# Attention and two feed-forward layers on one core: scores and P times V in one run each on TensorE, another order of first loads, a larger gap between weight tiles

## The chip, the core and the metric

The kernel runs on one core of a Trainium2 chip. Five engines work on their own queues, in order: TensorE (PE in the profile, with its weight loads as PEld), VectorE (DVE), ScalarE (ACT), GpSimd (POOL) and SyncE (SP), which here only issues DMAs. Times are device microseconds (us) of one execution. A comparison is between medians of several executions.

## What is computed

Sliding-window attention with a few global keys, a gated layer (w_in, w_out) and a second gated layer (w_gate, w_val, w_out). Batch 2, 8 heads, 768 tokens of 64 numbers per head; 1536 tokens of 512 numbers go through the layers. The reference, cut:

```python
def _attn_ref(q, k, v, n_global, n_local):
    scores = scale * np.matmul(q, k.transpose(0, 1, 3, 2))
    is_global = pos[None, :] < int(n_global)              # 8
    is_local = (rel >= 0) & (rel < int(n_local))          # 96
    keep = is_global | is_local
    scores = np.where(keep, scores + bias, -1000000000.0) # bias: slope of the head times distance
    a = np.exp(scores - np.max(scores, axis=-1, keepdims=True))
    a = a / (np.sum(a, axis=-1, keepdims=True) + 1e-09)
    return np.matmul(a, v)

def _moe_ref(x, w_in, w_out):
    h = x @ w_in
    return (h * (1.0 / (1.0 + np.exp(-h)))) @ w_out       # w_in 512 x 2048

def _moe2_ref(x, w_gate, w_val, w_out):
    gate = 1.0 / (1.0 + np.exp(-(x @ w_gate)))            # 512 x 1536
    return (gate * (x @ w_val)) @ w_out
```

The inputs are 64-bit numbers in memory; the kernel takes them as pairs of words or as 32-bit copies.

## The kernel before

**Attention.** Queries are cut into 12 blocks of 128 tokens (gi), each with four pairs of heads (p); n = 4 gi + p counts the pairs, and a slot m is two pairs, n = 2m and 2m + 1. Keys of a block and of the one before are all that a block needs. For a pair, `emit_T` transposes keys and queries on TensorE (L339) and copies them into kT on VectorE or ScalarE (L350, L352), with the head's scale. `emit_QK` multiplies queries and keys (L376): each head of the pair has 64 rows, so one head works in the upper and one in the lower half of the array's rows, into two PSUM banks. `soft` adds the mask and takes the maximum on VectorE (L391), the exponential on ScalarE (L398), divides by the sum (L404, L405 on VectorE, L407 on GpSimd). `emit_PT` transposes the result (L424) and copies it (L428). `emit_PV` multiplies with v (L445): each head has 64 columns of output, so the two heads work in two halves of the array's columns. Once all four pairs of a block are done, `take` copies the block into x as a high and a low part (L462 on ScalarE, L463 on VectorE) and issues the next load of v.

**Layers.** Products use the full array in three passes of high and low parts (`mm3`, L493, and L668, L670 later). Weights come as 64-bit numbers, 512 KB a tile, in three stage buffers (L173); `split_w` turns a tile into a high and a low part: L153 on ScalarE, L154, L155 and L158 on VectorE, L166 on ScalarE, L167 on VectorE. L155, L158 and L167 read two SBUF tiles. Sixteen weight tiles fit in at first.

**Order.** The program first runs the loads and masks (`load_qk`, `load_n`, `make_n`, `make_mask0`, `make_mask1`), then `run_att` with the first six slots of attention and no products, then `window`, which deals products and attention into each other by the table PLAN, then `phase_rest` with products alone. After each piece `unit` advances a counter; `pump_w` writes a `split_w` when at least `wst["gap"]` units (5) have passed since the last. What stands in the program is not yet the order on the engines: a scheduler takes all of it, keeps what depends on what, and fills each engine's queue in the order in which it estimates the inputs and the engine to be free, earlier program text first. In the first products (`window`) 256 tokens are done at a time: the first half needs the copies of blocks 0 and 1, the second half those of blocks 2 and 3.

In a head's first unit, `head`, the P times V of the slot two earlier come first and then the scores. Before, they were free pieces for the scheduler. While TensorE has nothing, `warm_up` multiplies zeros (L883) in the first 20 units.

Of the kernel before, what the change touches and what calls it, by code (L numbers as in the profile page):

```python
# [31 lines left out]
def attn_moe_moe2_kernel(  # L32
# [15 lines left out]
    B, H, S, D = q.shape  # L48
# [34 lines left out]
    def run_due():  # L83
        while True:
            due = [d for d in deferred if d[0] <= clock[0]]
            if not due:
                return
            d = min(due, key=lambda e: (e[0], e[1]))
            deferred.remove(d)
            d[2]()  # L90
# [7 lines left out]
    def unit():  # L98
        clock[0] += 1
        pump_w()  # L100
        run_due()
# [34 lines left out]
    wst = {"dma": 0, "split": 0, "on": False, "last": -100, "gap": 5, "wait": 8}  # L136
# [44 lines left out]
    def pump_w():  # L181
        if not wst["on"]:
            return
        n = wst["split"]
        if n < wst["dma"] and clock[0] >= wtime[n] + wst["wait"] and clock[0] >= wst["last"] + wst["gap"]:
            split_w(n)
            wst["split"] = n + 1
            wst["last"] = clock[0]
        n = wst["dma"]
        if n < len(wsrc) and n - wst["split"] < 3 and slot_free(n):  # L190
            dma_w(n)
            wst["dma"] = n + 1
# [27 lines left out]
    def load_n():  # L220
        raw = ap1.tile([128, 2, 2], I32, name="nraw")
        nc.sync.dma_start(out=raw[:, 0, :], in_=n_global.bitcast(I32).partition_broadcast(128))
        nc.scalar.dma_start(out=raw[:, 1, :], in_=n_local.bitcast(I32).partition_broadcast(128))
        return raw
# [73 lines left out]
    qk_t = {}  # L298
    v_t = {}

    def load_qk(gi):
        if gi >= NBLK:
            return
        b, s0 = gi // BLK, gi % BLK * 128
        t = qk_p.tile([128, 2, H, D], F32, tag="qk", name="qk")
        for h0, h1 in ((0, 2), (2, H)) if gi == 0 else ((0, H),):
            if gi == 0 and h0 == 2:
                qk_t["n"] = load_n()
            for j, src in enumerate((k, q)):
                eng = nc.scalar if gi == 0 and j else nc.sync  # L310
                eng.dma_start(
                    out=t[:, j, h0:h1], in_=src[b, h0:h1, s0:s0 + 128, :].rearrange("h p d -> p h d")
                )
        qk_t[gi] = t
# [16 lines left out]
    def emit_T(n):  # L331
# [28 lines left out]
        if p == NP - 1:  # L360
            load_qk(gi + 2)

    def emit_QK(n):
        gi, p = divmod(n, NP)
        if gi >= NBLK:
            return
        s, i = gi % 2, gi % BLK
        kt = kT[p]
        u, m = n % 2, n // 2
        sp = [bk["SA"][m % len(bk["SA"])], bk["SB"][m % len(bk["SB"])]]  # L370
        w = 128 if i == 0 else 256
        sp = [x[:, u * 256:u * 256 + w] for x in sp]
        for e in range(2):
            r = slice(64 * e, 64 * e + 64)
            rhs = kt[r, s, :] if i == 0 else kt[r, 0:2, :].rearrange("p a b -> p (a b)")
            nc.tensor.matmul(sp[e], kt[r, 2, :], rhs, start=True, stop=True)  # L376
        return sp

    def soft(n, sp):
        if sp is None:  # L380
            return
        gi, p = divmod(n, NP)
        s, i = gi % 2, gi % BLK
        w = 128 if i == 0 else 256
        t = t_p.tile([128, 2, 256], F32, tag="t", name="t")
        t_t[n] = t
        c = 2.0 ** -(2 * p + 1)
        m0 = 0 if i == 0 else (128 if s == 0 else 256)
        ss = ssum[n % 4]
        for e in range(2):  # L390
            nc.vector.tensor_tensor_reduce(  # L391
                t[:, e, 0:w], sp[e], mask[e][:, m0:m0 + w], op0=ALU.add, op1=ALU.min,
                scale=-c, scalar=3.0e38, accum_out=nm_all[:, gi, 2 * p + e:2 * p + e + 1],
            )

        def exps():
            for e in range(2):
                nc.scalar.activation(  # L398
                    out=t[:, e, 0:w], in_=t[:, e, 0:w], func=AF.Exp, scale=-1.0,
                    bias=nm_all[:, gi, 2 * p + e:2 * p + e + 1], accum_out=ss[:, e:e + 1],  # L400
                )

        def norm():
            nc.vector.tensor_scalar(ss, ss, 1.0e-9, None, op0=ALU.add)  # L404
            nc.vector.reciprocal(ss, ss)  # L405
            for e in range(2):
                nc.gpsimd.tensor_scalar(  # L407
                    t[:, e, 0:w], t[:, e, 0:w], ss[:, e:e + 1], 1.0, op0=ALU.mult, op1=ALU.mult
                )

        defer(1 + n % 2, exps)
        defer(2 + n % 2, norm)

    def emit_PT(n):
        gi, p = divmod(n, NP)
        if n < 0 or gi >= NBLK:
            return
        i = gi % BLK
        nk = 1 if i == 0 else 2
        t = t_t.pop(n)  # L420
        ps = bk["PT"][n % len(bk["PT"])]
        for e in range(2):
            for c in range(nk):
                nc.tensor.transpose(  # L424
                    ps[:, (e * nk + c) * 128:(e * nk + c + 1) * 128], t[:, e, c * 128:(c + 1) * 128], ident
                )
        pt = pt_p.tile([128, 512], F32, tag="pt", name="pt")
        nc.scalar.activation(out=pt[:, 0:256 * nk], in_=ps[:, 0:256 * nk], func=AF.Copy)  # L428
        pt_t[n] = pt

    def emit_PV(n):
        gi, p = divmod(n, NP)
        if n < 0 or gi >= NBLK:
            return
        s, i = gi % 2, gi % BLK
        pt = pt_t.pop(n)
        ps = bk["PV"][gi % len(bk["PV"])]
        if i == 0:
            vs = [v_t[gi]]
        else:  # L440
            vs = [v_t[gi], v_t[gi - 1]] if s == 0 else [v_t[gi - 1], v_t[gi]]
        nk = len(vs)
        for c in range(nk):
            for e in range(2):
                nc.tensor.matmul(  # L445
                    ps[64 * e:64 * e + 64, p * 128:(p + 1) * 128],
                    vs[c][:, (2 * p + e) * D:(2 * p + e + 1) * D],
                    pt[:, (e * nk + c) * 128:(e * nk + c + 1) * 128],
                    start=(c == 0),
                    stop=(c == nk - 1),  # L450
                )

    def take(n):
        gi, p = divmod(n, NP)
        if n < 0 or gi >= NBLK or p < NP - 1:
            return
        i = gi % BLK
        ps = bk["PV"][gi % len(bk["PV"])]
        g, j = divmod(gi, BPG)
        xs = slice(j * 128, (j + 1) * 128)  # L460
        pv = ps.rearrange("p (a b) -> p a b", a=NP)
        nc.scalar.activation(out=X[g][:, 0, :, xs], in_=pv, func=AF.Copy)  # L462
        nc.vector.tensor_tensor(X[g][:, 1, :, xs], pv, X[g][:, 0, :, xs].bitcast(F32), ALU.subtract)  # L463
        if 0 < i < BLK - 1:
            nc.sync.dma_start(
                out=v_t[gi][0:N_GLOB, :].rearrange("p (h d) -> p h d", h=H),
                in_=v[gi // BLK, :, 0:N_GLOB, :].rearrange("h p d -> p h d"),
            )
        load_v(gi + 2)

    def att_units(m0, m1):
        def head(n):
            emit_PV(n - 4)
            emit_PV(n - 3)
            sp = [emit_QK(n), emit_QK(n + 1)]
            take(n - 3)
            soft(n, sp[0])
            soft(n + 1, sp[1])

        for m in range(m0, m1):  # L480
            n = 2 * m
            yield lambda n=n: head(n)
            yield lambda n=n: emit_PT(n - 2)
            yield lambda n=n: emit_T(n + 2)
            yield lambda n=n: emit_PT(n - 1)
            yield lambda n=n: emit_T(n + 3)
# [122 lines left out]

    def run_att(n0, n1):  # L610
        wst["on"] = True
        for j, u in enumerate(att_units(n0, n1)):
            u()
            if j < 20:
                warm_up(1)
            unit()

    def phase_rest(prev):
        tasks = [("A1", NG - 1, c) for c in halves1[0]]
# [261 lines left out]
    def warm_up(n):  # L881
        for _ in range(n):
            nc.tensor.matmul(bank[4][:, 256:512], warm[:, 0:128], warm, start=True, stop=True)  # L883

    with ExitStack():
# [16 lines left out]
                  H=[bank[5], bank[6]], Y=[bank[7]])  # L902
# [45 lines left out]
```

## Time and profile before

| | us |
|---|---|
| median of three runs | 702.73 (699.41 to 702.90) |
| the profiled execution, whole | 700.78 |
| its span, first to last instruction | 698.9 |
| TensorE busy in the span | 680.9 |
| VectorE busy | 376.3 |
| ScalarE busy | 278.1 |
| GpSimd busy | 90.7 |

The profile's chain of waits is followed back from the last instruction: 93% of the span in it is TensorE. The time before the first product (41 us) is where TensorE has holes; the attention's slots then run until about 210 us beside products, and the rest is products. TensorE's figure of busy time counts matmuls that overlap, so two rows that both read 0.70 us may stand 0.63 apart; the distance from a start to the next start is the better measure, and the chain of waits gives it.

### The profile page before, as it was taken

How to read it: one execution, taken by the hardware profiler on the slowest of the kernel's cores; microseconds unless marked ns; L12 is line 12 of the kernel's file. 1: busy time of each engine (PE TensorE's matmuls, PEld its weight loads, DVE VectorE, ACT ScalarE, POOL GpSimd, SP SyncE). 2: the span in 40 equal slices, each digit the busy share in tenths (PEclk: the TensorE clock that was granted, in tenths of full speed). 3: DMA queues.
4: the chain of work that ended last, by engine and by line, in shares of the span. 5: the costliest groups of instructions: out<-in, count | busy, mean ns of one | idle time of the engine just before them, and what ended most of it. 6: DMA issues, size and time to landing. Idle time of an engine off the chain costs nothing.

```text
span 698.9 us, 9170 instructions
## 1 busy us (share of the span) xinstructions
PE 680.9 (97%) x3393; PEld 532.4 (76%) x3393; DVE 376.3 (54%) x861; ACT 278.1 (40%) x594; POOL 90.7 (13%) x174
## 2 busy tenths in 40 slices
PE   6899999999999999999999999999999999999995
PEld 4467776667767888888888888888888888888884
DVE  4899975635459999752389941311684211312212
ACT  3788755655446565432266521111352111111110
POOL 4455553342320000000000000000000000000000
PEclk9999999999999999999999999999999999999998
DMA  8676543110002554500025420000140000100101
GB/s 198 150 202 172 151 131 74 44 36 17 16 2 93 165 166 126 173 1 0 1 88 153 151 90 1 1 0 1 60 151 0 1 1 0 61 0 1 61 0 65
DMA packets 65268, 49.03 MB, mean 70 GB/s; under 512 B 39616, under 2 KB 60096, under 8 KB 65216
## 3 DMA queue, kind: packets, MB, share of 16 engines
q1 hardware_dynamic: 64016, 48.11, 24.0%
q8 instruction: 28, 0.46, 0.3%
q10 hardware_dynamic: 1200, 0.26, 0.2%
q14 instruction: 24, 0.20, 0.1%
HBM read 45.22 MB, written 3.15 MB: 69 GB/s over the span
## 4 chain that ended last, share of the span: by engine, by line
PE 93%; DVE 2%; ACT 2%; DMA 1%; issue 1%; POOL 0%; ACTq 0%; DVEq 0%
PE bank L493 55%; PE bank L670 14%; PE bank L668 13%; PE bank L376 4%; PE bank L445 3%; PE bank L424 3%; PE bank L339 2%; DMA nraw<-in_n_local_dram 1%; ACT t L398 1%; DVE t L391 0%; DVE acc L689 0%; ACT pt L428 0%; PE bank L883 0%; POOL t L407 0%; ACT u L153 0%
## 5 line engine op out<-in xcount | busy, mean ns | idle before, releaser
L493 PE MATMUL bank<-x,w 128*128 128x512 f32 (+1 forms) x1488 | 356.3, 389 | 0.6 <-ACT w L166 0.6
L493 PEld LDWEIGHTS bank<-x,w 128*128 128x128 f32 x1488 | 272.9, 188 | 65.7 <-issue 3.5
L530 DVE TENSOR_TENSOR sg<-sg,bank 128x512 f32<-128x512 f32 x36 | 24.7, 687 | 167.5 <-PE bank L493 167.5
L670 PE MATMUL bank<-w,g 128*128 128x512 f32 x432 | 104.5, 390 | 0.0
L670 PEld LDWEIGHTS bank<-w,g 128*128 128x128 f32 x432 | 81.1, 188 | 17.8
L668 PE MATMUL bank<-g,w 128*128 128x512 f32 x384 | 92.9, 390 | 0.0
L668 PEld LDWEIGHTS bank<-g,w 128*128 128x128 f32 x384 | 72.1, 188 | 15.9
L527 ACT ACTIVATE sg<-bank 128x512 f32<-128x512 f32 x36 | 21.5, 597 | 120.0 <-PE bank L493 119.9
L531 ACT ACTIVATE g<-sg 128x512 fp32r<-128x512 f32 x36 | 22.8, 633 | 93.1 <-DVE sg L530 93.1
L407 POOL TENSOR_SCALAR t<-t,ssum 128x256 f32<-128x256 f32 (+1 forms) x96 | 53.3, 573 | 42.0 <-DVE ssum L404 18.0
L493 PE MATMUL bank<-g,w 128*128 128x512 f32 (+1 forms) x240 | 55.0, 363 | 0.3 <-DVE acc L579 0.2
L166 ACT ACTIVATE w<-u 128x512 fp32r<-128x512 f32 x68 | 42.4, 630 | 32.1 <-DVE u L158 14.8
L153 ACT ACTIVATE u<-stage 128x512 f32<-128x512 f32 x68 | 45.3, 674 | 23.8 <-DVE w L167 18.7
L167 DVE TENSOR_TENSOR w<-u,w 128x512 fp32r<-128x512 f32 x68 | 46.5, 689 | 12.0 <-ACT w L166 11.7
L398 ACT ACTIVATE t<-t,nm_all 128x256 f32<-128x256 f32 (+1 forms) x96 | 46.1, 484 | 9.2 <-DVE nm_all L391 9.1
L155 DVE SCALAR_TENSOR_TENSOR u<-stage,u 128x512 int32<-128x512 int32 x68 | 48.7, 723 | 0.6
L158 DVE SCALAR_TENSOR_TENSOR u<-stage,u 128x512 int32<-128x512 int32 x68 | 47.9, 708 | 0.3
L493 PEld LDWEIGHTS bank<-g,w 128*128 128x128 f32 x240 | 37.9, 189 | 9.5 <-DVE acc L579 1.5
L391 DVE CUSTOM_DVE_ANT_0 t<-bank,mask 128x256 f32<-128x256 f32 (+1 forms) x96 | 33.3, 395 | 11.7 <-PE bank L376 10.3
L376 PE MATMUL bank<-kt 64*128 64x256 f32 (+1 forms) x192 | 37.0, 431 | 1.2 <-DVE kt L350 0.8
L518 ACT ACTIVATE g<-sg 128x512 fp32r<-128x512 f32 x48 | 30.2, 630 | 17.8 <-DVE sg L517 10.7
L517 DVE SCALAR_TENSOR_TENSOR sg<-sg,bank 128x512 f32<-128x512 f32 x32 | 21.9, 683 | 26.9 <-ACT sg L516 26.7
(89 smaller groups left out, 490.4 us busy)
## 6 DMA issues: line engine op xcount, KB each, us to landing
stage<-in_moe_w_out_dram SPq DMA_DIRECT2D x28, 512.0 KB, 4.0
stage<-in_moe_w_in_dram SPq DMA_DIRECT2D x16, 512.0 KB, 3.8
stage<-in_moe_w_gate_dram SPq DMA_DIRECT2D x12, 512.0 KB, 3.5
stage<-in_moe_w_val_dram SPq DMA_DIRECT2D x12, 512.0 KB, 3.5
v<-in_v_dram SPq DMA_DIRECT2D x12, 256.0 KB, 3.4
out_dram<-acc SPq DMA_DIRECT2D x12, 256.0 KB, 2.0
qk<-in_k_dram SPq DMA_DIRECT2D x11, 256.0 KB, 4.6
qk<-in_q_dram SPq DMA_DIRECT2D x11, 256.0 KB, 3.9
```

The lines of the kernel that those rows point to most:

```text
L153: nc.scalar.activation(out=st, in_=hw.bitcast(F32), func=AF.Copy, scale=2.0 ** -112)
L155: nc.vector.scalar_tensor_tensor(out=ui, in0=lw, scalar=29, in1=ui, op0=ALU.logical_shift_right, op1=ALU.bitwise_or)
L158: nc.vector.scalar_tensor_tensor(out=ui, in0=hw, scalar=-2 ** 31, in1=ui, op0=ALU.bitwise_and, op1=ALU.bitwise_or)
L166: nc.scalar.activation(out=w[:, 0, :], in_=st, func=AF.Copy)
L167: nc.vector.tensor_tensor(w[:, 1, :], st, w[:, 0, :].bitcast(F32), ALU.subtract)
L376: nc.tensor.matmul(sp[e], kt[r, 2, :], rhs, start=True, stop=True)
L391: nc.vector.tensor_tensor_reduce(t[:, e, 0:w], sp[e], mask[e][:, m0:m0 + w], op0=ALU.add, op1=ALU.min, scale=-c, scalar=3.0e38, accum_out= ...
L398: nc.scalar.activation(out=t[:, e, 0:w], in_=t[:, e, 0:w], func=AF.Exp, scale=-1.0, bias=nm_all[:, gi, 2 * p + e:2 * p + e + 1], accum_out ...
L407: nc.gpsimd.tensor_scalar(t[:, e, 0:w], t[:, e, 0:w], ss[:, e:e + 1], 1.0, op0=ALU.mult, op1=ALU.mult)
L493: nc.tensor.matmul(ps, wl[(slice(None), a) + wsl], xl[(slice(None), b) + xsl], start=(first and j == 0), stop=(last and j == len(order) - 1),)
L668: nc.tensor.matmul(yb[d], w[:, a, sl], gt[:, b, :], start=st, stop=en)
L670: nc.tensor.matmul(yb[d], gt[:, a, sl], w[:, b, :], start=st, stop=en)
```

## The change

Three edits. In `load_qk` the two word counts (n_global, n_local) are issued ahead of the first block's keys and queries, and these come in three pieces of heads (0 and 1, 2 and 3, 4 to 7) instead of two. In `head` the scores of both pairs and the P times V of two earlier pairs stand in a section in which the order on TensorE is the order of the text: scores of n + 1, scores of n, P times V of n - 3, P times V of n - 4. In `run_att` the gap between weight tiles is 9 units instead of 5.

```diff
--- before.py
+++ after.py
@@ load_qk
-        for h0, h1 in ((0, 2), (2, H)) if gi == 0 else ((0, H),):
-            if gi == 0 and h0 == 2:
-                qk_t["n"] = load_n()
+        if gi == 0:
+            qk_t["n"] = load_n()
+        for h0, h1 in ((0, 2), (2, 4), (4, H)) if gi == 0 else ((0, H),):
             for j, src in enumerate((k, q)):
                 eng = nc.scalar if gi == 0 and j else nc.sync
@@ att_units
         def head(n):
-            emit_PV(n - 4)
-            emit_PV(n - 3)
-            sp = [emit_QK(n), emit_QK(n + 1)]
+            with tc.manual_schedule(engines={mybir.EngineType.PE}):
+                sp = [emit_QK(n + 1), emit_QK(n)][::-1]
+                emit_PV(n - 3)
+                emit_PV(n - 4)
             take(n - 3)
@@ run_att
         wst["on"] = True
+        gap, wst["gap"] = wst["gap"], 9
         for j, u in enumerate(att_units(n0, n1)):
             u()
             if j < 20:
                 warm_up(1)
             unit()
+        wst["gap"] = gap
```

Three places in the queues show what moves. A row is a line of the program, the operation, output and inputs, and how many follow one another. kt_126 to kt_129 are the transposed keys and queries of head pairs 0 to 3; bank_76 and bank_77 take the scores of the two heads of a pair, bank_79 P times V; bank_78 and bank_80 the two kinds of transposes; x_87 is x for the first 512 tokens, w_93 to w_108 are the sixteen weight tiles, in the order of memory and not of use.

TensorE's queue in the first products, before:

```order
L424 MATMUL bank_78<-ident,t 128x128 x4
L445 MATMUL bank_79<-pt,v 64x128 x4
L493 MATMUL bank_82<-x_87,w_97 128x256 x7
L339 MATMUL bank_80<-ident,qk 128x128 x2
L376 MATMUL bank_76<-kt_126 128x256
L493 MATMUL bank_82<-x_87,w_97 128x256 x3
L493 MATMUL bank_82<-x_87,w_98 128x256 x8
L376 MATMUL bank_77<-kt_126 128x256
L493 MATMUL bank_82<-x_87,w_98 128x256 x4
L445 MATMUL bank_79<-pt,v 64x128 x4
L424 MATMUL bank_78<-ident,t 128x128 x4
```

The same stretch of TensorE's queue after:

```order
L494 MATMUL bank_82<-x_87,w_97 128x256 x9
L376 MATMUL bank_76<-kt_127 128x256
L376 MATMUL bank_77<-kt_127 128x256
L376 MATMUL bank_76<-kt_126 128x256
L376 MATMUL bank_77<-kt_126 128x256
L445 MATMUL bank_79<-pt,v 64x128 x8
L424 MATMUL bank_78<-ident,t 128x128 x4
L339 MATMUL bank_80<-ident,qk 128x128 x2
```

The scores of two pairs and the P times V of two pairs, each split up by products before, stand in one piece (x8 here is sixteen records of the profile, since each of these products makes two).

VectorE's queue around the copy of the first attention block into x (L463), before:

```order
L391 ISA t,nm_all<-bank_77,mask_125 128x256
L391 ISA nm_all 128x1
L167 TENSOR_TENSOR w_93<-u,w_93 128x512
L391 ISA t,nm_all<-bank_77,mask_125 128x256
L391 ISA nm_all 128x1
L350 TENSOR_SCALAR kt_129<-bank_80 128x256
L463 TENSOR_TENSOR x_87<-bank_79,x_87 128x4x128
```

And after:

```order
L154 TENSOR_SCALAR u<-u 128x512
L391 ISA t,nm_all<-bank_82,mask_125 128x256
L391 ISA nm_all 128x1
L391 ISA t,nm_all<-bank_82,mask_125 128x256
L391 ISA nm_all 128x1
L167 TENSOR_TENSOR w_97<-u,w_97 128x512
L155 SCALAR_TENSOR_TENSOR u<-stage,u 128x512
L463 TENSOR_TENSOR x_87<-bank_79,x_87 128x4x128
```

Before, the first weight tile (w_93) is finished just ahead of this copy; after, the fifth (w_97) is.

TensorE's queue up to the first product on tokens 256 to 511 (the last row but one before, the last row after), before:

```order
L376 MATMUL bank_77<-kt_129 128x256
L339 MATMUL bank_80<-ident,qk 128x128 x2
L445 MATMUL bank_79<-pt,v 64x128 x4
L424 MATMUL bank_78<-ident,t 128x128 x4
L493 MATMUL bank_83<-g,w_99 128x256 x3
L493 MATMUL bank_83<-g,w_100 128x256 x3
L493 MATMUL bank_83<-g,w_99 128x256 x3
L493 MATMUL bank_83<-g,w_100 128x256 x3
L339 MATMUL bank_80<-ident,qk 128x128 x2
L493 MATMUL bank_81<-x_87,w_93 128x256
L493 MATMUL bank_82<-x_87,w_97 128x256
```

And after:

```order
L376 MATMUL bank_77<-kt_128 128x256
L339 MATMUL bank_80<-ident,qk 128x128 x2
L445 MATMUL bank_79<-pt,v 64x128 x8
L424 MATMUL bank_78<-ident,t 128x128 x4
L339 MATMUL bank_80<-ident,qk 128x128 x2
L376 MATMUL bank_76<-kt_127 128x256
L376 MATMUL bank_77<-kt_127 128x256
L376 MATMUL bank_76<-kt_126 128x256
L376 MATMUL bank_77<-kt_126 128x256
L339 MATMUL bank_80<-ident,qk 128x128 x2
L494 MATMUL bank_81<-x_87,w_93 128x256
```

Before, twelve products of the half before stand between the block's last P times V and that product; after, those are done earlier, and a run of scores of the next slot stands there.

## Rows read from the trace of the kernel before

**Rows 1.** The page's first lines: span, busy time, share, instructions.

```profile
span 698.9 us, 9170 instructions
PE 680.9 (97%) x3393; PEld 532.4 (76%) x3393; DVE 376.3 (54%) x861; ACT 278.1 (40%) x594; POOL 90.7 (13%) x174
```

**Rows 2.** Busy time by windows: window, length, engines, TensorE clock, DMA share, GB/s.

```profile
20.00:30.00 10.00, 6.59 (x46) 3.71 (x46) 10.00 (x35) 7.72 (x24) 3.75 (x6) 0.97 0.63 161
...
42.00:60.00 18.00, 17.79 (x133) 13.65 (x133) 17.30 (x51) 14.95 (x40) 12.23 (x18) 1.00 0.65 184
60.00:80.00 20.00, 20.00 (x164) 15.44 (x163) 18.47 (x55) 15.18 (x39) 7.54 (x11) 1.00 0.56 154
...
100.00:120.00 20.00, 20.00 (x139) 14.44 (x138) 9.48 (x36) 9.82 (x29) 7.30 (x17) 1.00 0.36 85
```

**Rows 3.** Chain of waits, 42 to 71 us: start, length, engine, line, instructions.

```profile
43.92 1.02 PE bank L445 x16
...
48.08 0.63 PE bank L376 x4
...
50.51 0.59 PE bank L445 x8
...
52.35 0.63 PE bank L376 x2
...
66.55 0.37 PE bank L339 x2
...
68.09 1.44 PE bank L493 x12
69.53 0.22 PE bank L339 x2
69.75 0.23 PE bank L493 x2
```

**Rows 4.** VectorE's groups by line, 42 to 100 us: busy us, mean ns.

```profile
L155 DVE SCALAR_TENSOR_TENSOR u<-stage,u 128x512 int32<-128x512 int32 x12 | 10.7, 899 | 0.1
...
L158 DVE SCALAR_TENSOR_TENSOR u<-stage,u 128x512 int32<-128x512 int32 x12 | 9.9, 822 | 0.0
L167 DVE TENSOR_TENSOR w<-u,w 128x512 fp32r<-128x512 f32 x12 | 8.3, 690 | 0.0
```

**Rows 5.** The same view, 42 to 60 us.

```profile
L155 DVE SCALAR_TENSOR_TENSOR u<-stage,u 128x512 int32<-128x512 int32 x4 | 4.1, 1038 | 0.0
```

**Rows 6.** Timeline: start, length, engine, line, operation, output and input, idle before.

```profile
3.15 0.44 PEld L339 LDWEIGHTS bank<-ident,qk 128*128 128x128 f32 x2
...
10.65 0.28 DVE L391 CUSTOM_DVE_ANT_0 t<-bank,mask 128x128 f32<-128x128 f32 x1
...
18.16 0.49 DVE L154 TENSOR_SCALAR u<-u 128x512 int32<-128x512 int32 x1 [0.99 <-ACT u L153]
...
31.58 0.42 DVE L391 CUSTOM_DVE_ANT_0 t<-bank,mask 128x256 f32<-128x256 f32 x1 [1.53 <-PE bank L376]
...
38.04 0.75 DVE L154 TENSOR_SCALAR u<-u 128x512 int32<-128x512 int32 x2
...
39.65 0.67 DVE L155 SCALAR_TENSOR_TENSOR u<-stage,u 128x512 int32<-128x512 int32 x1
40.25 0.68 DVE L158 SCALAR_TENSOR_TENSOR u<-stage,u 128x512 int32<-128x512 int32 x1
...
57.12 1.28 POOL L520 TENSOR_TENSOR g<-sg,g 128x512 fp32r<-128x512 f32 x1
57.19 1.76 DVE L155 SCALAR_TENSOR_TENSOR u<-stage,u 128x512 int32<-128x512 int32 x1
...
69.69 0.68 DVE L463 TENSOR_TENSOR x<-bank,x 128x512 fp32r<-128x512 f32 x1
```

**Rows 7.** Chain of waits, first 12 us.

```profile
1.23 5.33 DMA nraw<-in_n_local_dram
...
6.66 0.18 DVE nf L229
```

## Prediction, before the changed kernel ran

> **What bounds the kernel now.** I read the page first, then the busy time by windows, then the chain of waits, then single rows of the timeline. The page has TensorE (PE) busy for 97% of the span [rows 1]; matmuls overlap in that figure, so the reader should look at what stands beside it. The windows [rows 2] show three stages. Early, TensorE has holes while VectorE is full (6.59 and 10.00 of 10 us from 20 to 30). From 42 us on TensorE is full (17.79 of 18, then 20.00 of 20), and up to 80 us VectorE nearly so (17.30 of 18, 18.47 of 20). After 100 us VectorE has half its time free (9.48 of 20) and TensorE alone is the bound. So time comes off in two ways: TensorE's queue needs less time for the same work, or the point from which it never waits again comes earlier. And early on a saving on TensorE can be eaten by VectorE, which has no room there.
>
> I cut the program at one point and call it S: the first product on tokens 256 to 511, which needs the fourth attention block (256 tokens are two blocks). In the chain it starts at 69.75 us [rows 3], as VectorE takes up that block's copy at 69.69 [rows 6]. Behind S I count TensorE work, ahead of S VectorE work.
>
> **Edit 1, the tied runs, behind S.** The scores use half of the array's rows, P times V half of its columns, and a change to or from the full array costs. In the chain [rows 3] eight P-times-V records take 0.59 us and sixteen in one run 1.02: the second eight cost 0.43, so entering and leaving costs 0.16 inside the run. The neighbours pay too: a pair of transposes takes 0.22 us, but 0.37 between two such runs, 0.15 more for one way out and one way in. A saved run of P times V is worth 0.16 + 0.15 = 0.31 us. A score pair takes 0.63 us; its two passes of 256 columns would stream in 0.43, by the rate of the second eight. So a saved run of scores is worth 0.20 + 0.15 = 0.35. A lone half of a pair (x2) also takes 0.63, as much as both halves (x4).
>
> In the order of TensorE's queue behind S there are 30 runs of scores before and 13 after, 34 runs of P times V before and 16 after. 17 x 0.35 = 5.95 and 18 x 0.31 = 5.58. Two pairs that were split are whole now: 0.43 and, for a pair of 128 columns, half of that. Some work has also moved ahead of S: 12 products of 256 columns (1.44 [rows 3]), two score pairs (0.86) and a transpose pair (0.22). Sum: **14.7 us less** on TensorE behind S. No run of two score pairs stands in the trace. If the second pair in a run cost 0.63 and not 0.43, the 13 runs would give 2.6 back and 12.1 would be left; I take 0.43, because the run of sixteen shows it for P times V. The number of instructions is the same.
>
> **Edit 1, ahead of S.** The P times V of a slot now stands behind the scores of the slot two later, in one fixed piece. What waits on it is the block's copy into x on ScalarE, and so the first products. In the scheduler's order this lets the weight tiles past: before the copy of the first, second, third and fourth block, VectorE finished 1, 4, 8 and 11 weight tiles; now it is 5, 10, 15 and 16. VectorE works in order, so what stands ahead of S has to be done. From its first weight instruction (18.16 [rows 6]) to the last one that S waits for, its queue holds the same 32 softmax instructions (L391), 8 key copies and 14 sums (L404) in both kernels, but now 6 more L154, 6 more L155, 7 more L158, 5 more L167 and 2 more L579. Starts of such 512-column instructions lie 0.60 apart (39.65 to 40.25), two L154 take 0.75 [rows 6]. 20 x 0.60 + 6 x 0.37 = **14.2 us more**. From below: VectorE's idle time up to S (1.53 at 31.58 [rows 6], 0.7 and half of 1.5 in [rows 2]) could take up 3.0 of it: 11.2. From above, with the means of 42 to 100 us [rows 4]: 6 x 0.37 + 6 x 0.90 + 7 x 0.82 + 7 x 0.69 = 18.2. I take 14.2, since the holes come from chains that stay.
>
> Also, S stood right behind the fourth block; now a tied run of scores, which waits for the last L391 counted above, and a transpose pair stand between: 0.63 + 0.43 + 0.37 = 1.4 us more.
>
> **Edit 2, the order of first loads.** The two word counts (n_global, n_local) were issued at 1.23 and took 5.33 us; the mask chain starts at 6.66 [rows 7] and the first softmax instruction at 10.65 [rows 6]. Now they are issued first, where the first keys were, 0.5 us earlier. In return the first keys and queries queue behind them, and with the third piece SP and ScalarE each issue one DMA more, ahead of the loads of v and of the second block. The softmax covers that: its first scores are needed only at 10.65, while their first transposes stood at 3.15 [rows 6]. If the counts landed as fast as those keys (2.4 us from issue to transpose), the masks would be 3.3 us earlier, and the second pair of heads, in a small piece of its own now, would be next late. I take **0.5 less**, range 0 to 3.3.
>
> **Edit 3, the larger gap** between weight tiles. With the first two edits in place, the rows of all five queues are the same with and without it: the scheduler starts tiles by what is free, not by where they were written. It doesn't do what it says and counts 0; before the copy that the first product needs, tiles rise from 4 to 10.
>
> **The sum.** -14.7 + 14.2 + 1.4 - 0.5 = +0.4 us on a span of 698.9 [rows 1]. Around the span lie 1.9 us in the profiled execution (700.78): 701.2. The median of the three runs shown is 702.73; 0.5% of it, 3.5 us, is about what a measurement of this kernel can tell from no change, so "same" is 699.2 to 706.2. I forecast **701.2, no difference**: what TensorE saves, VectorE takes back before S. With the bounds of the VectorE term it is 698.2 to 705.2.
>
> **Rivals.** *Weight work in the holes (faster).* VectorE's idle time takes up 3.0 us of the added work and the counts land early: 11.2 + 1.4 - 3.3 - 14.7 = -5.4, so 695.4. For it: idle time exists, and the new order was made for free time. Against it: VectorE is at 96% from 42 to 60 us already [rows 2]. Chance 0.28.
>
> *Tied blocks that starve VectorE (slower).* The piece of scores and P times V waits as a whole for its last input, everything behind it in TensorE's queue waits along, and VectorE stands before its softmax. That happened once, for 1.53 us at 31.58 [rows 6]. Eight slots (2 to 9) lie between the first weight instruction and S: 8 x 1.53 = 12.2, so 713.4. It decides the sign from 0.6 us each. Against it: VectorE has weight work to do meanwhile. Chance 0.15.
>
> *VectorE and GpSimd in each other's way (slower).* An L155 that began at 57.19 beside a GpSimd L520 took 1.76 us, where another took 0.67 [rows 6], and from 42 to 60 us L155 took 1.04 in the mean [rows 5]. 18 of the added instructions read two SBUF tiles, as L155 does; at 0.36 us each that is 6.5 more, so 707.7. It decides from 0.28 each. Against it: L158 and L167 show less of it (0.82 and 0.69 [rows 4]). Chance 0.11. The Trainium skill has a rule for it ("SBUF — State Buffer", section "SBUF: two separate sides"): a VectorE instruction with two SBUF inputs and a GpSimd instruction that reads SBUF take a shared port pair as an exclusive lock, and the loser blocks for the whole of the other. The row of 1.76 us agrees; the rule speaks against weight work pulled in beside the softmax, and by it most of the added instructions could pay.
>
> **How the numbers follow.** Forecast 0.46, rivals 0.28, 0.15, 0.11. A little of the forecast's own range lies below 699.2 and nothing above 706.2; of the GpSimd case the smaller half of its price is still "same". Faster 0.32, same 0.42, slower 0.26. The predicted time is the forecast's, 701.2. The range leaves out about 0.1 on either side, the far ends of the first and of the second rival: 693.5 to 708.5.
>
> **What would show it.** In the profile after: P-times-V rows of x16 at about 1.02 us, score rows of x8 at about 1.06 (1.26 refutes the 0.43). S at about 85 us, not 70. VectorE full from 18 to 80 us, and emptier than before from 85 to 100. The mask chain from about 6.1. From S to the end 14.7 us less. I am wrong if S comes before 80 us (faster), if VectorE stands idle for TensorE for over 5 us before S (slower), or if TensorE waits for more than 2 us between S and 215 us.

## The result, and the profile after

The changed kernel takes 709.34 us (median of four runs, 708.42 to 710.90) against 702.82 for the kernel before beside it: 1.0112 times, 95% interval 1.0086 to 1.0138. It is slower by 1.1%; the forecast was no difference. The profiled execution after took 710.9 us with a span of 709.1. It is the slowest of its four, while the one before (700.78) is below its median, so the two spans differ by 10.2 us where the medians differ by 6.5. In lines behind L470 the numbers are one to three higher than before (L493 is L494, L577 to L579 are L578 to L580).

Three numbers split the loss. From here on S, the first product on tokens 256 to 511, is its start in the timeline, which can be read in every kernel (before: 69.50; the chain's row is 0.25 later).

| | before | after | forecast for after |
|---|---|---|---|
| S | 69.50 | 90.17 | 84.6 |
| from S to the end of the span | 629.4 | 618.9 | 614.7 |
| span | 698.9 | 709.1 | 699.3 |

So of the 9.8 us between the forecast and this execution, 5.6 were lost ahead of S and 4.2 behind it. A profiled execution of no_gap, below, which is the same program, has S at 88.83 and 617.6 behind it: 4.2 lost ahead of S and 2.9 behind it.

The page's first lines after, beside [rows 1]: TensorE and VectorE are busy for 4 to 5 us *less* than before, in a span that is 10 us longer. What was added is waiting, not work.

```profile
span 709.1 us, 9161 instructions
PE 675.9 (95%) x3393; PEld 537.9 (76%) x3393; DVE 372.2 (52%) x861; ACT 279.7 (39%) x594; POOL 88.3 (12%) x174
```

The windows after, beside [rows 2] (window, length, busy us of each engine with instructions, TensorE clock, DMA share, GB/s):

```profile
20.00:30.00 10.00, 7.13 (x33) 4.00 (x31) 9.08 (x26) 6.93 (x18) 4.17 (x6) 1.00 0.70 199
42.00:60.00 18.00, 12.71 (x84) 9.34 (x83) 14.79 (x45) 12.61 (x33) 6.37 (x10) 0.81 0.63 178
60.00:80.00 20.00, 16.26 (x141) 13.49 (x138) 17.66 (x49) 14.02 (x35) 9.50 (x14) 1.00 0.58 159
80.00:100.00 20.00, 17.27 (x160) 14.37 (x159) 12.62 (x54) 12.82 (x41) 8.88 (x20) 1.00 0.49 120
100.00:120.00 20.00, 20.00 (x155) 17.00 (x154) 9.28 (x38) 11.10 (x33) 7.61 (x14) 1.00 0.19 41
```

Look at 42 to 60 us. I expected VectorE (third figure of the five) to be full there; it has 3.2 us free, TensorE has 5.3 us free and ScalarE 5.4. No engine is full in this stretch, so steps that pass from engine to engine must set a part of its length. TensorE's granted clock is below full there too (0.81 in the mean).

VectorE's window from its first weight instruction to S, before and then after:

```profile
18.16:69.50 51.34, 47.31 (x357) 32.81 (x356) 48.23 (x153) 41.79 (x113) 27.95 (x47) 0.97 0.66 174
```

```profile
17.14:90.17 73.03, 56.27 (x384) 40.49 (x383) 63.85 (x185) 49.85 (x129) 32.55 (x52) 0.95 0.63 173
```

VectorE's work in it grew from 48.2 to 63.9 us, by 15.6. The forecast had 14.2 for it; its further 1.4 was for rows of TensorE just ahead of S. The instructions that it counted came, and a key copy (L350), a copy into x (L463) and two more sums with them. VectorE's idle time grew from 3.1 to 9.2, by 6.1, which the forecast had at nothing. The window began 1.0 earlier.

Where the idle time lies is in the timeline after (start, length, engine, line, operation; in brackets the idle time before and what ended it):

```profile
45.09 0.21 DVE L405 RECIPROCAL ssum<-ssum 128x2 f32<-128x2 f32 x2
45.76 3.33 POOL L407 TENSOR_SCALAR t<-t,ssum 128x256 f32<-128x256 f32 x4 [4.08 <-DVE u L154]
48.23 1.15 PE L424 MATMUL bank<-ident,t 128*128 128x128 f32 x4 [0.79 <-POOL t L407]
48.96 0.60 ACT L428 ACTIVATE pt<-bank 128x512 f32<-128x512 f32 x1 [2.52 <-PE bank L424]
49.45 0.62 ACT L166 ACTIVATE w<-u 128x512 fp32r<-128x512 f32 x1
50.10 0.69 DVE L167 TENSOR_TENSOR w<-u,w 128x512 fp32r<-128x512 f32 x1 [2.19 <-ACT w L166]
...
61.83 0.67 ACT L153 ACTIVATE u<-stage 128x512 f32<-128x512 f32 x1 [2.67 <-DMA stage<-in_moe_w_in_dram]
62.54 0.43 DVE L154 TENSOR_SCALAR u<-u 128x512 int32<-128x512 int32 x1 [2.02 <-ACT u L153]
...
88.36 0.17 DVE L404 TENSOR_SCALAR ssum<-ssum 128x2 f32<-128x2 f32 x1 [0.95 <-ACT t L398]
...
88.91 1.14 PE L376 MATMUL bank<-kt 64*128 64x256 f32 x8 [0.90 <-DVE kt L350]
```

The first six rows are one round trip. The sums of the softmax (L404, L405) stand between weight steps in VectorE's queue; GpSimd has waited 4.08 us when it divides (L407; the row names L154 as what ended the wait, while by the program L407 needs the L405 just ahead); the transposes on TensorE (L424) and the copy on ScalarE (L428) come after it, and behind that copy, in ScalarE's queue, stands L166 of a weight tile, for which VectorE then waits 2.19. The next two rows are a weight tile that isn't there yet: its transfer started when VectorE had freed the stage buffer (L158 in the chain below) and took 5.54 us, and VectorE waits 2.02. These two places are 4.2 of the 9.2 us of idle time. In all VectorE waits 5.0 us for these two kinds of ScalarE steps (L153, L166) inside its window (2.19, 2.02 and 0.79), 0.3 before: 4.7 of the 6.1. The last two rows stand just ahead of S: the run of scores there did not wait for the last L391, as the forecast had it, but 0.90 us for a key copy, which stood in VectorE's queue behind a sum that had waited 0.95.

The chain of waits after, beside [rows 3, 7]:

```profile
0.72 4.14 DMA nraw<-in_n_local_dram
4.88 0.18 DVE nf L229
...
55.55 0.61 DVE u L158
56.21 5.54 DMA stage<-in_moe_w_in_dram
...
88.91 1.14 PE bank L376 x8
90.05 0.37 PE bank L339 x2
90.42 0.24 PE bank L494 x2
...
95.22 1.02 PE bank L445 x16
96.24 0.59 PE bank L424 x4
96.83 1.06 PE bank L376 x8
```

The word counts land 1.8 us earlier than in [rows 7]. The tied runs are as long as forecast: 1.02 for sixteen P-times-V records, 1.06 for two pairs of scores (1.26 would have refuted the 0.43 for the second pair). A tied run of scores and two transposes stand ahead of S. And the GpSimd contention that one rival built on did not grow: VectorE's groups from 42 to 100 us, beside [rows 4] (mean ns of one is the last figure but one), are shorter than before, 753 for 899 and 732 for 822.

```profile
L155 DVE SCALAR_TENSOR_TENSOR u<-stage,u 128x512 int32<-128x512 int32 x10 | 7.4, 753 | 0.0
L158 DVE SCALAR_TENSOR_TENSOR u<-stage,u 128x512 int32<-128x512 int32 x10 | 7.2, 732 | 0.0
```

TensorE's waits after, from S to 240 us (us in total, times, longest): 2.2 us, where the kernel before has 0.2.

```profile
PE bank L494 <- DVE acc L580: 1.4, 4, 0.3
PE bank L376 <- DVE ssum L404: 0.6, 1, 0.6
PE bank L494 <- ACT x L462: 0.2, 1, 0.2
```

### The profile page after: what moved, and what is told of

It is laid out like the page before. It is cut to its first block, busy times and chain, and to the rows that moved or that the text cites. A ratio compares the mean times of both kernels' runs of the same rounds, so it can differ in the third digit from the quotient of the medians.

```text
span 709.1 us, 9161 instructions
## 1 busy us (share of the span) xinstructions
PE 675.9 (95%) x3393; PEld 537.9 (76%) x3393; DVE 372.2 (52%) x861; ACT 279.7 (39%) x594; POOL 88.3 (12%) x174
## 4 chain that ended last, share of the span: by engine, by line
PE 87%; DVE 7%; ACT 2%; DMA 1%; issue 1%; POOL 1%; DVEq 0%; ACTq 0%; SPq 0%
PE bank L494 53%; PE bank L673 14%; PE bank L671 12%; PE bank L376 3%; PE bank L424 2%; PE bank L445 2%; DVE t L391 1%; DVE u L158 1%; DVE u L155 1%; ACT t L398 1%; PE bank L339 1%; DMA stage<-in_moe_w_in_dram 1%; DVE acc L580 1%; DVE w L167 1%; POOL t L407 1%
## 5 line engine op out<-in xcount | busy, mean ns | idle before, releaser
L494 PE MATMUL bank<-x,w 128*128 128x512 f32 (+1 forms) x1488 | 352.9, 388 | 1.2 <-DVE x L463 0.6
L494 PEld LDWEIGHTS bank<-x,w 128*128 128x128 f32 x1488 | 272.7, 188 | 62.8 <-ACT x L462 1.0
L407 POOL TENSOR_SCALAR t<-t,ssum 128x256 f32<-128x256 f32 (+1 forms) x96 | 52.7, 565 | 80.7 <-DVE ssum L405 48.1
L494 PE MATMUL bank<-g,w 128*128 128x512 f32 (+1 forms) x240 | 53.6, 360 | 5.1 <-DVE acc L580 3.4
L153 ACT ACTIVATE u<-stage 128x512 f32<-128x512 f32 x68 | 45.7, 674 | 29.2 <-DVE w L167 25.6
L166 ACT ACTIVATE w<-u 128x512 fp32r<-128x512 f32 x68 | 42.6, 631 | 29.9 <-DVE u L158 12.6
L155 DVE SCALAR_TENSOR_TENSOR u<-stage,u 128x512 int32<-128x512 int32 x68 | 47.6, 701 | 0.8
L158 DVE SCALAR_TENSOR_TENSOR u<-stage,u 128x512 int32<-128x512 int32 x68 | 47.2, 696 | 0.3
L494 PEld LDWEIGHTS bank<-g,w 128*128 128x128 f32 x240 | 37.7, 189 | 12.7 <-DVE acc L580 5.5
L391 DVE CUSTOM_DVE_ANT_0 t<-bank,mask 128x256 f32<-128x256 f32 (+1 forms) x96 | 33.8, 398 | 23.1 <-PE bank L376 16.8
L424 PE MATMUL bank<-ident,t 128*128 128x128 f32 x176 | 32.8, 303 | 5.1 <-POOL t L407 3.9
```

Of the source, the lines that this page charges most:

```text
L153: nc.scalar.activation(out=st, in_=hw.bitcast(F32), func=AF.Copy, scale=2.0 ** -112)
L155: nc.vector.scalar_tensor_tensor(out=ui, in0=lw, scalar=29, in1=ui, op0=ALU.logical_shift_right, op1=ALU.bitwise_or)
L158: nc.vector.scalar_tensor_tensor(out=ui, in0=hw, scalar=-2 ** 31, in1=ui, op0=ALU.bitwise_and, op1=ALU.bitwise_or)
L166: nc.scalar.activation(out=w[:, 0, :], in_=st, func=AF.Copy)
L391: nc.vector.tensor_tensor_reduce(t[:, e, 0:w], sp[e], mask[e][:, m0:m0 + w], op0=ALU.add, op1=ALU.min, scale=-c, scalar=3.0e38, accum_out= ...
L407: nc.gpsimd.tensor_scalar(t[:, e, 0:w], t[:, e, 0:w], ss[:, e:e + 1], 1.0, op0=ALU.mult, op1=ALU.mult)
```

## The experiments

**Theories.** A: the order within the tied section (P times V behind the scores) lets weight tiles past the attention on VectorE, and what VectorE has to do ahead of S, with the round trips that stand between it, sets S. B: a tied section waits as a whole, so it starves the engines in each slot before S, whatever the weights do. C, a sharper form of A: it is not the tying but the place of P times V behind the scores. D: the half clock of TensorE around 45 to 52 us is a part of it.

All with the shared runs of the kernel before; the ratio is to those. "Tiles" are the weight tiles VectorE has finished at the copies of the first four blocks.

| kernel | tiles | S | S to end | median us | ratio, 95% interval |
|---|---|---|---|---|---|
| before | 1, 4, 8, 11 | 69.5 | 629.4 | 702.8 | 1 |
| changed | 5, 10, 15, 16 | 90.2 | 618.9 | 709.34 | 1.0112 (1.0086 to 1.0138) |
| tie_alone | 5, 9, 14, 16 | 85.8 | 619.3 | 706.85 | 1.0077 (1.0050 to 1.0105) |
| loads_alone | 0, 4, 8, 11 | 73.5 | 626.9 | 699.46 | 0.9972 (0.9952 to 0.9991) |
| hold_weights | 2, 5, 8, 11 | 78.1 | 621.0 | 701.15 | 0.9991 (0.9971 to 1.0010) |
| tie_late | 0, 4, 8, 11 | 73.3 | 619.5 | 693.04 | 0.9875 (0.9842 to 0.9909) |
| tie_early | 5, 10, 15, 16 | 89.4 | 625.3 | 716.78 | 1.0215 (1.0198 to 1.0232) |
| pv_first | 0, 5, 9, 13 | 75.0 | 621.6 | 700.88 | 0.9993 (0.9974 to 1.0012) |
| more_warm | 5, 10, 15, 16 | 88.0 | 618.0 | 707.50 | 1.0080 (1.0063 to 1.0096) |
| mix | 0, 5, 9, 13 | 74.7 | 623.1 | 699.62 | 0.9976 (0.9960 to 0.9993) |
| half_weights | 3, 7, 11, 15 | 71.5 | 617.6 | 690.56 | 0.9842 (0.9819 to 0.9865) |
| tie_late_old_loads | 1, 4, 8, 11 | 70.5 | 622.1 | 693.94 | 0.9886 (0.9862 to 0.9910) |
| tie_from_9 | 0, 4, 8, 11 | 72.0 | 617.9 | 692.40 | 0.9885 (0.9846 to 0.9924) |
| no_gap | 5, 10, 15, 16 | 88.8 | 617.6 | 708.92 | 1.0112 (1.0085 to 1.0138) |

The kernel before has medians of 701.40, 702.12 and 701.54 us in the runs beside these kernels. S and the time behind it are read from one profiled execution each, and the two executions of one program (changed, no_gap) differ by 1.3 us in either. The profiled ones of loads_alone (702.21) and tie_late (694.59) are the slowest of theirs, that of pv_first (698.48) the fastest of its ten.

### The parts alone: tie_alone, loads_alone, no_gap

tie_alone is the second hunk of the change without the others, loads_alone the first, no_gap all but the third.

> The kernel before with the tied section alone (no new order of loads, gap 5). Both theories have the loss in the tied section, so: S (first product on tokens 256 to 511) at about 92 us, since the 1.4 us of the earlier start are gone, and 710 to 712 us. If instead the new order of loads is what hurts (other transfers late), S is under 85 and the time under 703.

> The kernel before with the new order of first loads alone. The mask chain started 1.8 us earlier and the first softmax 1.4 us earlier in the changed kernel, so if nothing else is moved: S at 68.3 and 701.3 us. If the start is absorbed behind it: 702.8. If the later keys and queries hurt: over 704.

> The changed kernel with the third edit undone (gap 5 instead of 9). The rows of all five queues are those of the changed kernel, so both theories: 707 to 710 us, S at 90 as there. A difference of more than 3 us would mean that something beyond the order of the queues counts.

The tied section alone is slower than before, as expected, but by less: 706.85 us with S at 85.8, not 92. The loads alone gain 0.28%, and not where I looked for it: in the profiled execution S comes 4 us *later* than before and 2.5 us less is left behind it, since the order of the queues moves too. With the tied section they don't gain, they lose: tie_alone and no_gap differ in the order of the loads alone, and have medians of 706.85 (706.33 to 707.88) and 708.92 us (708.26 to 710.47). no_gap is the changed kernel again, as the equal rows of the queues said. By the medians most of the loss is in the tied section, the rest in the two edits together.

VectorE's window in tie_alone, to hold against that of the changed kernel above:

```profile
17.06:85.75 68.69, 52.51 (x378) 39.76 (x376) 64.58 (x191) 49.51 (x133) 30.66 (x50) 0.85 0.67 178
```

Its work there is as long as in the changed kernel (64.6 us for 63.9), and nearly as many tiles pass the copies. But its idle time is 4.1 us, not 9.2; it waits 0.2 us for L153 and L166, not 5.0. In the three other kernels that tie the early slots in the changed kernel's way with the new order of loads and all of the weight work, idle time is 7.6 (no_gap), 8.8 (tie_early) and 6.8 (more_warm). So the tied section brings the added work by itself, and most of the added idle time comes only when the new order of loads stands beside it. Why it comes then was not tried and stays open.

### Which slots: tie_late, tie_early, tie_late_old_loads, tie_from_9

```diff
-            with tc.manual_schedule(engines={mybir.EngineType.PE}):
-                sp = [emit_QK(n + 1), emit_QK(n)][::-1]
-                emit_PV(n - 3)
-                emit_PV(n - 4)
+            if n >= 20:
+                with tc.manual_schedule(engines={mybir.EngineType.PE}):
+                    sp = [emit_QK(n + 1), emit_QK(n)][::-1]
+                    emit_PV(n - 3)
+                    emit_PV(n - 4)
+            else:
+                emit_PV(n - 4)
+                emit_PV(n - 3)
+                sp = [emit_QK(n), emit_QK(n + 1)]
```

tie_early has `n < 20` in its place, tie_from_9 `n >= 18`; tie_late_old_loads is tie_late without the new order of loads.

> New order of loads, and the tied section only from slot 10 on (n >= 20), behind S; before S the order is free as in the kernel before. A and B alike: S at 68 to 70 us. Behind S TensorE's rows need about 10 us less than in the kernel before, so 690 to 692 us. If TensorE's waits behind S in the changed kernel come from the tied section itself and not from late weights, 2 to 4 us of that are lost and it is 693 to 696.

> The counterpart of tie_late: new order of loads, the tied section only up to slot 9 (n < 20), free order behind it. If the loss is made before S and nothing behind S depends on it: S at 88 to 91 us, from S to the end about 627 us as in loads_alone, 716 to 718 us. If the loss in the changed kernel came partly from behind S, less: 710 to 713.

> tie_late with the order of first loads of the kernel before: the tied section from slot 10 on is the only edit. In the kernel before S is at 69.5 us with 629.4 us behind it; 16 runs of scores and 18 of P times V fewer give 11.2 less and the waits seen in tie_late 1.6 more: S at 69.5 and 690 to 692 us for the whole. If the new order of loads adds its 0.3% here as it does alone, it is 2 us slower than tie_late: 695 us.

> tie_late with one slot more tied: from slot 9 (n >= 18), whose section holds the last P times V that the fourth block's copy needs, behind the scores. If the place of P times V behind scores costs per slot what the early slots show (tie_early: 15.9 us over the slots up to 9), about 1.5 to 2 us of S are lost and TensorE saves two runs (0.7): 694 to 695 us. If a single slot is harmless: 692 to 693.

The loss is made ahead of S and the gain behind it, and they can be had apart. tie_early has S at 89.4 and takes 716.78 us, as expected; tie_late has S where loads_alone has it (73.3, not the 68 to 70 that I expected), and takes 693.04, faster than both kernels by over 1%. tie_late_old_loads came out at 693.94, 2 to 4 us above the first of my two numbers and 1 below the second, and tie_from_9 at 692.40: with the section late, neither the order of the loads nor one slot more can be told from nothing.

These kernels also measure the price of a run. loads_alone and tie_late issue the same TensorE instructions behind S, but tie_late has 11 runs of scores and 17 of P times V fewer. By the forecast's prices that is 11 x 0.35 + 17 x 0.31 = 9.1 us; measured are 626.9 - 619.5 = 7.4, and TensorE waits 1.6 longer there (2.4 for 0.8), so 9.0. tie_late_old_loads stands to the kernel before in the same way: 16 and 18 runs fewer, 11.2 by the prices; measured 7.3, and 3.5 more of waits: 10.8. Its waits from S to 240 us (L499 and L585 are L493 and L579 there):

```profile
PE bank L499 <- ACT x L462: 1.0, 1, 1.0
PE bank L424 <- ACT pt L428: 0.9, 1, 0.9
PE bank L424 <- POOL t L407: 0.9, 3, 0.4
PE bank L445 <- ACT pt L428: 0.3, 1, 0.3
PE bank L499 <- DVE acc L585: 0.3, 1, 0.3
PE bank L339 <- ACT kt L352: 0.3, 1, 0.3
```

The price of a run held, as far as single executions can tell, in which the time behind S can differ by 1.3 us. What didn't hold is that TensorE behind S waits for nothing: a shorter queue on TensorE runs into steps of other engines that it used to cover, for 1.6 to 3.5 us.

### What ahead of S: hold_weights, half_weights, pv_first

In hold_weights a weight tile's scratch is first touched by ScalarE, with one column of x from the attention block before the last one taken (blocks 0 to 3), so its steps can't be put ahead of that block's copy:

```diff
+        hb = wst.get("tk", -1) - 1
+        if hb >= 0:
+            nc.scalar.activation(
+                out=st[:, 0:1], in_=X[hb // BPG][:, 0, 0, hb % BPG * 128:hb % BPG * 128 + 1].bitcast(F32), func=AF.Copy
+            )
         to_f32(st, stages.pop(n))
```

> The changed kernel, and ScalarE writes one column into the scratch tile of a weight tile from x of a finished attention block before it works on the tile. The output is the same. By the queues VectorE then finishes 2, 5, 8 and 11 weight tiles before the copies of the first four blocks (5, 10, 15, 16 in the changed kernel), with all runs still tied. Theory A (weight tiles pulled ahead of S are what costs): S at 69 to 73 us and 690 to 694 us, faster than both kernels. Theory B (a tied section that waits as a whole starves the engines in each slot before S, whatever the weights do): S stays beyond 83 us, 703 us or more.

half_weights takes away work:

```diff
-    def to_f32(st, raw):
+    def to_f32(st, raw, n=512):
-            out=ui, in0=lw, scalar=29, in1=ui, ...
+            out=ui[:, 0:n], in0=lw[:, 0:n], scalar=29, in1=ui[:, 0:n], ...
-            out=ui, in0=hw, scalar=-2 ** 31, in1=ui, ...
+            out=ui[:, 0:n], in0=hw[:, 0:n], scalar=-2 ** 31, in1=ui[:, 0:n], ...
-        to_f32(st, stages.pop(n))
+        to_f32(st, stages.pop(n), 256 if n < 16 else 512)
```

> The changed kernel, but for the first sixteen weight tiles the two merging steps on VectorE (L155, L158) work on 256 of 512 columns, so half of each tile is not put together and the output is not the reference's. VectorE then has 32 x 0.30 = 9.6 us less ahead of S, and by the queues 3, 7, 11, 15 tiles before the first four copies, one tile (about 2 us) fewer ahead of S. Theory A (what VectorE has queued ahead of S sets S): S 9 to 12 us earlier, at 78 to 81, and 697 to 700 us. Theory B (the tied sections and the chains between engines set S, and VectorE's work only fills the waits): S at 86 us or later, 705 us or more.

pv_first changes the order inside the section:

```diff
             with tc.manual_schedule(engines={mybir.EngineType.PE}):
-                sp = [emit_QK(n + 1), emit_QK(n)][::-1]
-                emit_PV(n - 3)
                 emit_PV(n - 4)
+                emit_PV(n - 3)
+                sp = [emit_QK(n), emit_QK(n + 1)]
```

> New order of loads, tied everywhere, but in the order P times V of n - 4 and n - 3, then the scores of n and n + 1. By the queues VectorE finishes 0, 5, 9 and 13 tiles before the first four copies, near the 0, 4, 8, 11 of loads_alone; on TensorE the scores still stand in runs of two pairs, but P times V in runs of one. Theory C (P times V behind the scores is what holds the copies back and lets the tiles past): S at 73 to 76 us; behind S 10 runs of scores fewer than in loads_alone at 0.35 us, less 1 to 2 us of waits: 697 to 699 us. Theory B (any fixed order starves the engines before S): S beyond 79 us and 703 us or more.

VectorE's windows from the first weight instruction to S, for hold_weights, half_weights, pv_first and, to compare, loads_alone:

```profile
17.14:78.14 61.00, 49.08 (x374) 38.14 (x372) 50.90 (x156) 43.90 (x126) 26.27 (x49) 0.94 0.56 146
```

```profile
17.12:71.51 54.39, 46.43 (x385) 35.66 (x383) 52.57 (x178) 47.75 (x128) 25.52 (x50) 1.00 0.73 197
```

```profile
17.78:75.01 57.23, 47.32 (x362) 35.33 (x360) 51.91 (x155) 43.66 (x113) 27.78 (x45) 0.91 0.62 166
```

```profile
18.82:73.52 54.70, 49.67 (x372) 34.50 (x368) 48.98 (x158) 42.56 (x117) 26.43 (x46) 0.94 0.56 151
```

With the tiles held back S comes 12.0 us earlier than in the changed kernel, and VectorE has 13.0 us less work in its window: A, with every run still tied. By the medians 8.2 us of it are left (701.15 for 709.34). But it doesn't come back to the 73.5 of loads_alone: VectorE's idle time is 10.1, not 5.7. With the tiles held it has nothing else to do while the late P times V goes its way; the first block's copy (ScalarE's part) is at 31.0 us, 23.3 in loads_alone. VectorE waits 5.1 us for scores from TensorE here (4.0 in loads_alone), so with the weight work held back the second rival's mark, over 5 us, is reached. So it is neither of my two numbers, 690 or 703: about 12 us of the shift go with the weight work, and 4.6 are left, for which the longer way from scores to copy is the likely reason; the column that ScalarE must wait for could be a part of it.

half_weights says the same from the other side, and more strongly than I expected. VectorE's work falls by 11.3 us, near what I put; its idle time falls by 7.4 as well, to 1.8 us, and S comes at 71.5, with all sections tied. So the idle time of the changed kernel isn't the tied section waiting as a whole, as B has it. It goes away with half of the merging work, but tie_alone has all of that work and 4.1 us of idle time, so the work isn't enough to bring it. TensorE's clock is at full in this window too (1.00 for 0.95), and this run can't tell the two apart.

pv_first keeps all sections tied, and with P times V first S is at 75.0, inside the 73 to 76 that C gave; the tiles stay behind the copies. The median, 700.88, is 2 us above what I expected; the profiled execution, 698.48, from which S is read, is within it and the fastest of the ten.

### Two that told less: more_warm, mix

more_warm has `if j < 40` for `if j < 20` in `run_att`; mix is pv_first's order up to slot 9 and the changed kernel's from slot 10 on.

> The changed kernel with a warm-up product in all 30 units of the run ahead of the window instead of 20, so TensorE has fewer empty stretches between 35 and 53 us, where its clock was at half from 45.3 to 52.1. Theory D (the half clock is a part of the loss): no half-clock stretch there and S 1 to 3 us earlier, 706 to 708 us. If VectorE's queue and its holes set S: S at 90 and 709 us, whatever the clock does.

> New order of loads, tied in the order of pv_first up to slot 9 and in the order of the changed kernel from slot 10 on. By theory C it has the early copies of pv_first and the late runs of tie_late: S at 73 to 76 us, from S to the end 618 to 620 us, 692 to 696 us. If fixed order as such costs before S it is slower than tie_late by as much as S is later.

more_warm gave the 707.5 us that D foresaw, and S at 88.0, but not by D's cause: TensorE's granted clock was at half (1.2 of 2.4 GHz) for as long as in the changed kernel, from 45 to 52 us. What the warm-up products moved stays open; S is 0.8 us from that of no_gap. no_gap, the same program as the changed kernel, says a part about the clock. From 26 to 55 us, and around the half clock, the changed kernel and then no_gap:

```profile
26.00:55.00 29.00, 21.18 (x109) 13.24 (x108) 24.81 (x69) 19.44 (x50) 13.08 (x18) 0.88 0.69 191
45.30:52.10 6.80, 5.24 (x24) 3.12 (x26) 3.84 (x9) 3.52 (x8) 3.75 (x6) 0.50 0.86 226
```

```profile
26.00:55.00 29.00, 20.27 (x109) 13.02 (x109) 25.66 (x72) 19.91 (x51) 13.04 (x17) 0.65 0.71 192
43.00:54.00 11.00, 7.77 (x38) 5.14 (x38) 8.05 (x25) 7.54 (x21) 3.76 (x6) 0.53 0.68 182
```

In this execution TensorE had a mean clock of 0.65 from 26 to 55 us, not 0.88, and S came at 88.8, not later than 90.2. So the further half clock, ahead of 45 us and behind 52, cost nothing that can be seen. D itself is not refuted: between 45 and 52 us the clock is at half in both executions, and VectorE's wait of 2.19 us lies there. The four transposes in that round trip took 1.15 us, and four at full clock take 0.66 (at 61.60 in the same timeline), so about 0.5 of the 2.19 us could be the clock's, by an estimate from these rows. No run here has the changed kernel's order with the full clock at that place.

mix has S at 74.7, as expected, but 623.1 behind it, where tie_late has 619.5, and its median, 699.62, is 3.6 us above the 692 to 696 I had put. It has 5 runs of scores more there (18 for 13) and two pairs of scores that in tie_late lie ahead of S: 5 x 0.35 + 2 x 0.43 = 2.6 of the 3.6. The rest of its distance from tie_late is not settled.

## Why the prediction was wrong, step by step

**VectorE's added work ahead of S** was sized well: 14.2 forecast, 15.6 measured. hold_weights takes it away and gets 12 us of S back. The run of scores ahead of S, which I had waiting for the last L391, waited for a later key copy; two sums, a key copy and a copy into x that I had not counted lie in the window with it.

**The holes** are the step that failed. I wrote that they come from chains that stay, and gave them no term; VectorE's idle time ahead of S grew by 6.1 us (4.5 in no_gap). The chains didn't stay: where VectorE waits longest, a weight step on ScalarE stands behind a copy of the softmax (2.19 us), and a weight tile's transfer has started late and runs long (2.02). The added work alone doesn't do it. In tie_alone, which has all of it, the holes grow by 1.0 us, and S is at 85.8, where the forecast's terms without the loads give 69.5 + 14.2 + 1.4 = 85.1. So the holes could be left out for the tied section by itself, and not for the tied section together with the new order of loads: the sum took the edits one by one. tie_alone's window is that of one execution; its median is below that of no_gap too. What in the two together opens the holes stays open.

The first rival had the sign the wrong way round (that weight work would fill the holes). The second (tied sections that starve VectorE for TensorE) had the sign right, but not the wait: VectorE's waits for TensorE's scores up to S are 1.9 us, 1.5 before, and half_weights has 1.8 us of idle time in all with every section tied. My mark for it, over 5 us of waiting for TensorE, wasn't reached in the changed kernel; the longest waits were for ScalarE, which waited for others.

**TensorE behind S** was to save 14.7 and saved 10.5 (11.8 in no_gap). The price of the runs, 11.5 of it, held in two other pairs of kernels (9.0 for 9.1, 10.8 for 11.2). Two things were wrong beside it. TensorE's waits, which I had at nothing, rose by 2.0. And of the 3.2 for whole pairs and for work moved ahead of S, 10.5 + 2.0 - 11.5 = 1.0 can be seen, by no_gap 2.3. Why the rest isn't there is not settled.

**The loads** were to give 0.5 with a range to 3.3. The masks start 1.8 earlier, and alone the edit gives 0.1 to 0.5%. But the first weight step, 1.0 earlier than before, is as early in tie_alone (17.06) and later in loads_alone (18.82), so it isn't the loads that move it; and beside the tied section they cost 2.1 us by the medians of tie_alone and no_gap, where I had a gain.

**The gap** does nothing, as said: 708.92 for 709.34 us.

**The GpSimd case** didn't happen: the means of L155 and L158 fell.

Put together: 15.6 + 6.1 - 1.0 later at S and 10.5 less behind it make +10.2 us of span, 698.9 to 709.1 in the profiled executions; by the medians the loss is 6.5. The forecast's mechanism, a gain on TensorE that VectorE takes back before S, was right as far as the work goes. It left out the waits, on VectorE ahead of S and on TensorE behind it, and they turn the balance.

## What to carry over

A saving on the engine that bounds the whole belongs in the stage where it bounds. Here the same edit costs 14 to 17 us in the slots where VectorE is nearly full (tie_early to loads_alone, by the spans and by the medians) and gains 6 to 8 in those where TensorE is (tie_late to loads_alone), and in the second stage alone it makes the kernel over 1% faster. If an order lets independent work past a chain on an in-order engine, count that work and also what the chain's own steps on that engine then wait for. Edits that each move the queues don't add up term by term: here the new loads gain alone and lose beside the tied section. And a queue that gets shorter uncovers waits: here 1.6 to 3.5 us.

## What the runs showed of the chip that I had not expected

TensorE's granted clock in the early stage differs from one execution of the same program to the next (0.88 and 0.65 in the mean from 26 to 55 us), and the execution with the lower clock has the earlier S (88.8 for 90.2 us). A run of scores (half of the array's rows) costs 0.35 us beyond its passes and a run of P times V (half of its columns) 0.31, the neighbours' share included; as differences of whole kernels, with TensorE's waits taken out, these prices came back as 9.0 for 9.1 and 10.8 for 11.2, where two executions of one program can differ by 1.3. A transfer of a 512 KB weight tile, with the next one issued 0.6 us later, took 5.54 us, where the median to landing of such tiles from 20 to 90 us is 4.1 to 4.3.
